# A schedule model with a clock for the load queue, an earlier start of the exponentials and a reordered tail, in a two-attention kernel

## Chip, cores, metric

The kernel runs on one core of one Trainium2 chip. The metric is device microseconds (us) of one execution, median over several; lower is better. Engines: PE is TensorE's matmul and PEld its weight load, ACT is ScalarE, DVE is VectorE, POOL is GpSimd, SP is SyncE, which issues most DMAs.

## The reference

Two independent attentions over 2048 tokens, width 512, 32 heads of 16; the two outputs are concatenated.

```python
# A: attention with a compressive memory, in 4 segments of 512 tokens
phi = lambda t: jnp.where(t > 0, t + 1.0, jnp.exp(t))
g = _sigmoid(beta).reshape(1, H, 1, 1)             # one gate per head
for s in range(N):
    logits = qs @ ks^T * scale + causal_mask       # within the segment
    a_dot = softmax(logits) @ vs
    a_mem = (phi(qs) @ M) / (phi(qs) @ z + 1e-6)   # memory of earlier segments
    outs.append(g * a_mem + (1.0 - g) * a_dot)
    M, z = M + phi(ks)^T @ vs, z + sum(phi(ks))
# B: plain attention, all 2048 keys, no mask; then a @ wo_a and b @ wo_b, concatenated
```
(Shortened: the einsums are written as products.)

## The kernel before

The stream that matters is: scores on PE into two alternating PSUM tiles (`s_ps`, of 3 and 2 banks) → exponential on ACT (`pT`, 749 tiles) → causal mask on GpSimd where needed → accumulation on PE (`acc`). A further 124 blocks of exponentials go to DVE (`vx`). All other work, called chores (projections, phi, memory products, normalisation, output), is fitted into that stream by a Python scheduler *while the program is being built*. It keeps a clock for each engine (`T`), and with it decides which instruction is written next; each engine then runs them in that order. So a constant of the model, such as `SWITCH` (us that PE loses between kinds of matmul), can change the order of the program.

```python
SWITCH = 0.095
ARRIVE = dict(wv=13.0, wk=15.3, wq=16.5, xb=(20.5, 26.0, 31.5, 37.0), wvb=24.0)
T = dict(pe=0.0, act=0.0, dve=0.0, pool=0.0)
# ...
def load_beta():                                   # the gate's 32 numbers
    bsrc = A_beta.rearrange("(rt j e) -> j rt e", j=4, e=2)
    for j in range(4):
        nc.scalar.dma_start(out=beta_t[32 * j:32 * j + 32, :].rearrange("p (rt e) -> p rt e", e=2),
                          in_=bsrc[j:j + 1].to_broadcast([32, 4, 2]))
# ... head: first weights and x are on their way
load_beta()
ld(nc.sync, 2)                                     # A's value weights, then the rest of its key and query weights
ld(nc.sync, 1, P)
ld(nc.sync, 0, P)
# ... first key and query projection, then
pin(nc.scalar.activation(gcol[:], beta_t[:], ACT.Exp, scale=-1.0))     # the gate exp: waits for beta
pin(nc.scalar.copy(kA[0, 0][:], ps0[0][:]))                            # the first scores wait for this
# ... the main loop
    if now >= rel - 0.03 and not held_back(t):
        scores(t)
        t += 1
        if t == 3:
            later(1.2, gates, prio=1)
        continue
# ... chores with due times; for a key of B:
chore(pos0["b", 0, rt] - LEAD + 3 * ch, counted("k", do_k(...)), after=ARRIVE["xb"][ch], ...)
# ... transposes of phi(k) on SP's queue, modelled as a fixed delay
held["pk"] = T["dve"] + 6.5
chore(d - 3, mem(), 2, after=T["dve"] + 7)
# ... tail
partial(3, ...); partial(2, ...)                   # B's last output: 3 of 4 products, in advance
while len(pvq) > 1:
    assert pv(1, True)                             # accumulations
partial(0, last[:, 0, :])
assert pv(1, True)
partial(1, last[:, 1, :])
# ... 4 transposes OT_b, each with the fourth product
# ... checks: are all softmax sums in range? -> flag; then 4 output copies and DMAs
# ... every engine loads the flag and branches over an exact path
```

## Time and profile before

902.71 us, median of 3 (902.5 to 904.79); the profiled execution, another one of 901.82 us, spans 900.1 us.

The page of the kernel before: the span, each engine's busy time with its share, and the group of the exponentials (line, engine, operation, output and input with shapes, count; busy us, mean ns; idle time ahead of it and what ended most of that).

```profile
span 900.1 us, 18954 instructions
...
PE 866.8 (96%) x7674; PEld 260.2 (29%) x7674; DVE 794.2 (88%) x1359; ACT 868.2 (96%) x779; POOL 152.1 (17%) x327
...
L827 ACT ACTIVATE pT<-s_ps 128x1536 bf16<-128x1536 f32 x749 | 856.8, 1287 | 8.3 <-PE s_ps L109 6.1
```

ACT and PE both show 96%. But 411 of PE's matmuls only fill with zeros, so ACT's exponentials are what bounds the kernel, and time can be won where ACT stands idle. The next view shows where it does: ACT's timeline in the first 30 us (start, duration of a run of like instructions, engine, line, operation, count; in brackets the idle time before it and what ended it).

```profile
13.02 0.21 ACT L1066 ACTIVATE gcol<-beta_t 128x8 f32<-128x8 bf16 x1 [9.66 <-DMA beta_t<-in_A_beta_dram]
13.13 0.57 ACT L1067 CAST kA<-k_ps 128x512 bf16<-128x512 f32 x1
14.41 2.37 ACT L827 ACTIVATE pT<-s_ps 128x1536 bf16<-128x1536 f32 x2 [0.71 <-PE s_ps L109]
18.05 4.74 ACT L827 ACTIVATE pT<-s_ps 128x1536 bf16<-128x1536 f32 x4 [1.27 <-PE s_ps L109]
...
28.21 2.37 ACT L827 ACTIVATE pT<-s_ps 128x1536 bf16<-128x1536 f32 x2 [1.62 <-PE s_ps L109]
```

The gate exp, which needs beta, stands in front of the key copy in ACT's order, and so ACT stands idle for 9.66 us and all scores wait with it, for a load of 64 bytes of data. (Not all of it is lost: PE ends the first projections, which the copy needs too, at about 9.0.) The first exp tile starts at 14.41 and, after more gaps, the ninth at 28.21.

After that ACT hardly rests. The same kernel in wide windows: the window, its length, then busy us (and count) of PE, PEld, DVE, ACT and POOL, granted clock, DMA share and GB/s; the last line sums 30 to 880 us.

```profile
90.00:200.00 110.00, 108.11 (x932) 32.77 (x931) 95.47 (x171) 109.14 (x100) 24.38 (x49) 1.00 0.06 13
...
sum 850.00, PE 833.56 PEld 249.40 DVE 774.57 ACT 846.62 POOL 139.16; mean PE 119.08 PEld 35.63 DVE 110.65 ACT 120.95 POOL 19.88
```

ACT is busy 846.62 of 850 us. The end is a chain of its own. First the last output copies and the flag, in the timeline, then two groups of the branch line (count, duration min/median/max in ns, first and last start in us).

```profile
892.69 0.14 DVE L1175 TENSOR_SCALAR flag<-f_ps 1x1 int32<-1x1 f32 x1 [0.26 <-PE f_ps L109]
892.76 1.29 DVE L1179 CAST osb<-l_ps 128x512 bf16<-128x512 f32 x2
```

```profile
L1294 SPq EVENT_SEMAPHORE  x8: 17/17/17, 898.2 to 898.7; - x8
...
L1294 PEldq COMPARE_BRANCH  x1: 3986/3986/3986, 893.6 to 893.6; - x1
```

The flag comes first, then the last two output copies; PE's branch takes 3.99 us, from 893.6 to 897.6, and the end follows.

### The profile page before, as it was taken

What the parts mean: (1) busy time and instruction counts of PE and PEld (TensorE: products, weight loads), DVE (VectorE), ACT (ScalarE), POOL (GpSimd) and SP (SyncE); (2) the same over time, 40 slices, a digit from 0 to 9 for tenths busy, and PEclk for the clock granted to TensorE, in tenths of its full rate; (3) what the DMA queues carried; (4) which work ended last, traced back from release to release, by engine and by line L of the source; (5) the groups of instructions that cost most, each with busy time, mean ns of one, the idle gap of its engine ahead of it and who ended that gap; (6) DMA issues with size and microseconds to landing.
All of it is one profiled execution on the core that took longest, in us unless ns stands there. A gap on an engine that the chain in (4) does not pass through costs nothing.

```text
span 900.1 us, 18954 instructions
## 1 busy us (share of the span) xinstructions
PE 866.8 (96%) x7674; PEld 260.2 (29%) x7674; DVE 794.2 (88%) x1359; ACT 868.2 (96%) x779; POOL 152.1 (17%) x327
## 2 busy tenths in 40 slices
PE   6999999999999999999999999999999999999996
PEld 2222222232323223222232223223222222222321
DVE  1777789989898998988989999999999899999995
ACT  3899999999999999999999999999999999999994
POOL 4630120411303003030120304002030300000000
PEclk8999999999999999999999999999999999999998
DMA  7700000010000110000000010000000000000001
GB/s 185 143 13 7 24 4 5 7 25 7 7 1 14 36 30 8 1 1 7 1 7 2 25 30 1 1 1 1 2 2 1 19 30 1 2 1 2 1 2 28
DMA packets 35649, 15.47 MB, mean 17 GB/s; under 512 B 27360, under 2 KB 35552, under 8 KB 35552
## 3 DMA queue, kind: packets, MB, share of 16 engines
q1 hardware_dynamic: 33776, 13.78, 6.5%
q8 instruction: 62, 1.02, 0.5%
q10 hardware_dynamic: 1776, 0.40, 0.2%
q14 instruction: 35, 0.29, 0.1%
HBM read 4.20 MB, written 4.19 MB: 9 GB/s over the span
## 4 chain that ended last, share of the span: by engine, by line
PE 42%; ACT 31%; issue 12%; DVE 5%; POOL 2%; DVEq 0%; ACTq 0%; POOLq 0%
ACT pT L827 30%; PE acc L109 19%; PE s_ps L109 11%; PE v_ps L109 7%; POOL pT L837 2%; DVE vx L899 2%; PE o_ps L109 2%; PE k_ps L109 1%; DVE vx L915 1%; ACT ex L284 1%; PE q_ps L109 1%; PE am_ps L109 0%; DVE tT L358 0%; DVE tN L391 0%; POOL qB L259 0%
## 5 line engine op out<-in xcount | busy, mean ns | idle before, releaser
L827 ACT ACTIVATE pT<-s_ps 128x1536 bf16<-128x1536 f32 x749 | 856.8, 1287 | 8.3 <-PE s_ps L109 6.1
L899 DVE TENSOR_SCALAR vx<-v_ps 128x512 uint16<-128x512 f32 x496 | 324.7, 684 | 30.2 <-PE v_ps L109 23.8
L109 PE MATMUL s_ps<-qB,KB 32*128 32x512 bf16 x1552 | 250.7, 382 | 8.9 <-ACT pT L827 5.5
L915 DVE TENSOR_SCALAR vx<-vx 128x2048 uint16<-128x2048 uint16 x372 | 244.6, 690 | 1.9 <-PE acc L109 0.7
L109 PE MATMUL acc<-vx,VB 128*32 128x512 f16 x1984 | 181.3, 385 | 0.6 <-DVE vx L915 0.3
L109 PE MATMUL v_ps<-qB,KB 32*128 32x512 bf16 x496 | 171.4, 382 | 1.1 <-DVE vx L899 0.5
L837 POOL TENSOR_SCALAR_AFFINE_SELECT pT<-pT 128x256 bf16<-128x256 bf16 (+2 forms) x242 | 104.8, 462 | 306.0 <-ACT pT L827 304.7
L109 PE MATMUL acc<-pT,VB 128*32 128x512 bf16 x1552 | 152.8, 387 | 0.0
L109 PEld LDWEIGHTS <-KB 32*128 32x128 bf16 x2048 | 84.2, 91 | 235.8 <-issue 227.8
L109 PE MATMUL acc<-zeros 128*128 128x512 bf16 x411 | 137.1, 386 | 0.0
L109 PEld LDWEIGHTS <-VB 128*32 128x32 bf16 x3536 | 74.5, 94 | 161.7 <-issue 152.4
L109 PE MATMUL s_ps<-qA,kA 32*128 32x384 bf16 (+3 forms) x512 | 54.1, 303 | 7.7 <-ACT kA L1067 4.7
L109 PEld LDWEIGHTS <-zeros 128*128 128x128 bf16 x433 | 35.1, 98 | 84.9 <-issue 77.0
L259 POOL TENSOR_SCALAR qA<-qc,par 128x512 bf16<-128x512 bf16 x24 | 16.5, 701 | 248.6 <-DVE qc L257 248.6
L358 DVE STREAM_TRANSPOSE tT<-acc 128x512 f32<-128x512 f32 x64 | 45.0, 704 | 10.2 <-PE acc L109 9.9
L109 PE MATMUL acc<-pT,vA 128*32 128x256 bf16 (+3 forms) x512 | 32.5, 305 | 1.2 <-DVE vx L899 0.8
L109 PEld LDWEIGHTS <-kA 32*128 32x128 bf16 x512 | 17.1, 92 | 47.8 <-issue 39.7
L259 POOL TENSOR_SCALAR qB<-qc,par 128x512 bf16<-128x512 bf16 x32 | 23.6, 750 | 8.6 <-DVE qc L257 8.6
L435 DVE CAST osb<-o_ps 128x512 bf16<-128x512 f32 x28 | 19.2, 687 | 6.6 <-PE o_ps L109 6.3
L304 DVE CAST vA<-v_ps 128x512 bf16<-128x512 f32 x16 | 11.0, 689 | 11.7 <-PE v_ps L109 11.7
L257 DVE CAST qc<-q_ps 128x512 bf16<-128x512 f32 x28 | 19.2, 684 | 2.4 <-PE q_ps L109 2.1
L109 PE MATMUL k_ps<-xT_a,w_a 128*128 128x512 bf16 x64 | 19.6, 383 | 0.8 <-DMA xT_a<-in_A_x_dram 0.7
(88 smaller groups left out, 419.1 us busy)
## 6 DMA issues: line engine op xcount, KB each, us to landing
out_dram<-osb SPq DMA_DIRECT2D x31, 128.0 KB, 1.7
w_b<-in_B_wqkv_dram SPq DMA_DIRECT2D x3, 512.0 KB, 5.2
phk<-phkT SPq DMA_TRANSPOSE x48, 2.3
w_a<-in_A_wv_dram SPq DMA_DIRECT2D x1, 512.0 KB, 6.6
wo_a<-in_A_wo_dram SPq DMA_DIRECT2D x1, 512.0 KB, 4.3
wo_b<-in_B_wo_dram SPq DMA_DIRECT2D x1, 512.0 KB, 5.1
w_a<-in_A_wk_dram SPq DMA_DIRECT2D x1, 384.0 KB, 7.9
w_a<-in_A_wq_dram SPq DMA_DIRECT2D x1, 384.0 KB, 8.5
```

What stands on the lines that cost most here:

```text
L109: return pin(nc.tensor.matmul(out, lhsT, rhs, **k))
L257: pin(nc.vector.tensor_copy(qc[:], ps[:]))
L259: pin(nc.gpsimd.tensor_scalar(dst[:, e, :], qc[:], par[:, e:e + 1], 0.0, ALU.mult, ALU.add))
L284: pin(nc.scalar.activation(ex[:], src, ACT.Exp))
L304: pin(nc.vector.tensor_copy(dst, ps[:].rearrange("p (h d) -> p h d", d=DH)))
L358: pin(nc.vector.transpose(st["tT"][:, e].rearrange("p c d -> p (c d)"), acc[:]))
L435: pin(nc.vector.tensor_copy(osb[:], ps[:]))
L827: pin(nc.scalar.activation(pT[:, 0:n, :], pt[:, 0:n, :], ACT.Exp, scale=SCALE))
L837: pin(nc.gpsimd.affine_select(out=blk, in_=blk, compare_op=ALU.is_ge, fill=0.0, base=0, pattern=[[0, len(sls)], [1, P]], channel_multiplie ...
L899: pin(nc.vector.tensor_scalar(x[:, j, :], vt[:], XSCALE, float(LADDER[0]), ALU.mult, ALU.add))
L915: pin(nc.vector.tensor_scalar(p[:], x[:], float(off - LADDER[0]), 32767.0, ALU.add, ALU.min))
```

## The change

Its intent: give the scheduler a clock for SP's load queue, so that phi of keys and projections wait for the transposes they need rather than for a fixed delay (`T["sp"]`, `on_sp`); make the key projections of B, except those of its first row tile, due 6 tile places earlier (`KLEAD`); give DVE fewer exponentials when it is behind (`VLATE`); let a normalisation go to GpSimd when the model allows; load beta once, contiguous and behind all of A's weights, and put the gate exp behind six exp tiles; load the second row tile's key and query weights ahead of the value weights; in the tail, put all partial output products ahead of the last two accumulations, and the checks behind the output copies.

```diff
-ARRIVE = dict(wv=13.0, wk=15.3, wq=16.5, xb=(20.5, 26.0, 31.5, 37.0), wvb=24.0)
+ARRIVE = dict(w1=11.0, wv=13.5, wk=16.0, wq=17.0, xb=(20.0, 27.0, 33.0, 39.0), wvb=23.0)
-    T = dict(pe=0.0, act=0.0, dve=0.0, pool=0.0)
+    T = dict(pe=0.0, act=0.0, dve=0.0, pool=0.0, sp=SPLOADS)
@@ load_beta
-        for j in range(4):
-            nc.scalar.dma_start(out=beta_t[32 * j:32 * j + 32, :]...)
+        nc.sync.dma_start(out=beta_a[:], in_=A_beta.partition_broadcast(P))
+    def spread_beta():                     # four small copies on GpSimd, beta_a -> beta_t
@@ head: order of loads
-        load_beta()
-        ld(nc.sync, 2)
-        ld(nc.sync, 1, P)
-        ld(nc.sync, 0, P)
+        ld(nc.sync, 1, P, 2 * P)
+        ld(nc.sync, 0, P, 2 * P)
+        ld(nc.sync, 2)
+        ld(nc.sync, 1, 2 * P)
+        ld(nc.sync, 0, 2 * P)
+        load_beta()
@@ projections of A, phi of keys
-                rel = T["pe"] + 10
+                rel = T["sp"] + 3.5
-                held["pk"] = T["dve"] + 6.5
+                held["pk"] = T["sp"] + 2.0
-                chore(d - 3, mem(), 2, after=T["dve"] + 7)
+                chore(d - 3, mem(), 2, after=T["sp"] + 2.5)
@@ keys of B
-                    chore(pos0["b", 0, rt] - LEAD + 3 * ch,
+                    chore(pos0["b", 0, rt] - LEAD - (KLEAD if rt else 0) + 3 * ch,
@@ blocks of exponentials for DVE
+            vmin = VMIN + VLATE * (max(0.0, T["dve"] - T["pe"]) + sum(t["us"] for t in tasks)) / QUAD
-                if u["name"] == "a" or len(u["kbs"]) < VMIN:
+                if u["name"] == "a" or len(u["kbs"]) < vmin:
@@ gate
-        pin(nc.scalar.activation(gcol[:], beta_t[:], ACT.Exp, scale=-1.0))
         pin(nc.scalar.copy(kA[0, 0][:], ps0[0][:]))
-                if t == 3:
-                    later(1.2, gates, prio=1)
+                if t == 6:
+                    pin(nc.scalar.activation(gcol[:], beta_t[:], ACT.Exp, scale=-1.0))
+                    later(1.2, gates, prio=1, ready=on_act(0.2, T["pe"]))
@@ tail
+        (partial 3, 2; accumulations until 2 are left; partial 0, 1; the last 2 accumulations)
-        (checks, flag)          # ahead of the four output copies
+        (checks, flag)          # behind them
@@ ... cut: use of the arrival time w1, GpSimd normalisation, guard on one buffer, bookkeeping of the clocks
```

More of the change, by code (lines that the diff above doesn't have):

```diff
@@ L41 @@
 VMIN = 3
+VLATE = 0.5
 VBACK = 1.5
@@ L58 @@
 POOLMIN = 99
+SPLOADS = 38.0
+SPTRANS = 1.45
+TAILPV = 2
+POOLTT = 1.2
+POOLSLACK = -99.0
+POOLWITH = 1.2
+POOLWAIT = 4.0
 LEAD = 2.5
+KLEAD = 6
 URGENT = 0.0
 START = 8.4
-ARRIVE = dict(wv=13.0, wk=15.3, wq=16.5, xb=(20.5, 26.0, 31.5, 37.0), wvb=24.0)
+ARRIVE = dict(w1=11.0, wv=13.5, wk=16.0, wq=17.0, xb=(20.0, 27.0, 33.0, 39.0), wvb=23.0)
 @with_exitstack
@@ L95 @@
     ports = {k: deque(maxlen=8) for k in ("dve", "pool")}
-    held = {"tT": False, "ex": False, "qc": 0, "phi": deque()}
+    held = {"tT": False, "aT": False, "ex": False, "qc": 0, "phi": deque()}
     def mm(out, lhsT, rhs, at=0.0, **k):
@@ L148, in palloc, with on_sp @@
         return t
+    def on_sp(us, ready):
+        T["sp"] = max(T["sp"], ready) + us
     def mark(key, at=None):
@@ L169 @@
     bd = const.tile([P, 2, P], F32, name="bd")
+    beta_a = const.tile([P, H], BF16, name="beta_a")
     beta_t = const.tile([P, 8], BF16, name="beta_t")
@@ L179, in load_beta @@
     def load_beta():
-        bsrc = A_beta.rearrange("(rt j e) -> j rt e", j=4, e=2)
+        nc.sync.dma_start(out=beta_a[:], in_=A_beta.partition_broadcast(P))
+    def spread_beta():
         for j in range(4):
-            nc.scalar.dma_start(out=beta_t[32 * j:32 * j + 32, :].rearrange("p (rt e) -> p rt e", e=2),
-                              in_=bsrc[j:j + 1].to_broadcast([32, 4, 2]))
+            q = slice(32 * j, 32 * j + 32)
+            pin(nc.gpsimd.tensor_copy(beta_t[q, :].rearrange("p (rt e) -> p rt e", e=2),
+                                      beta_a[q, :].rearrange("p (rt j e) -> p rt j e", j=4, e=2)[:, :, j, :]))
     def head_masks():
@@ L315, in move @@
                 nc.sync.dma_start_transpose(ph[:, kb, :], pk[:, kb * P:(kb + 1) * P])
+            on_sp(4 * SPTRANS, T["dve"] + 0.1)
             if then is not None:
@@ L368, in f @@
             if "aT" not in st:
+                held["aT"] = live[0]
                 st["aT"] = wk.tile([P, 2, 16, 32], F32, name="aT", tag="aT")
@@ L372, in f @@
                 then()
-        later(0.72, f, am)
+        later(0.72, f, am, ok=lambda: "aT" in st if e else not held["aT"])
     def fin_pair(wk, st, name, rt, ridx, ot):
@@ L389, in fin_pair @@
         if aT is None:
-            yield -0.75
-            pin(nc.vector.tensor_tensor(o, tT[:, :, :, 0:DH], rr.to_broadcast(bc), op=ALU.mult))
+            eng = (yield (POOLTT, 0.75)) or nc.vector
+            pin(eng.tensor_tensor(o, tT[:, :, :, 0:DH], rr.to_broadcast(bc), op=ALU.mult))
         else:
@@ L397, in fin_pair @@
             t1, t2 = tT[:, :, :, 0:DH], aT[:, :, :, 0:DH]
-            yield -0.7
-            pin(nc.vector.tensor_tensor(t1, t1, rr.to_broadcast(bc), op=ALU.mult))
-            yield -0.7
-            pin(nc.vector.tensor_tensor(t2, t2, r2[:].to_broadcast(bc), op=ALU.mult))
-            yield -0.7
-            pin(nc.vector.tensor_tensor(o, t1, t2, op=ALU.add))
+            eng = (yield (POOLTT, 0.7)) or nc.vector
+            pin(eng.tensor_tensor(t1, t1, rr.to_broadcast(bc), op=ALU.mult))
+            eng = (yield (POOLTT, 0.7)) or nc.vector
+            pin(eng.tensor_tensor(t2, t2, r2[:].to_broadcast(bc), op=ALU.mult))
+            eng = (yield (POOLTT, 0.7)) or nc.vector
+            pin(eng.tensor_tensor(o, t1, t2, op=ALU.add))
         yield 0.71
@@ L437, in evac @@
             nc.sync.dma_start(out=out2[r0:r0 + P, col0[name]:col0[name] + D], in_=osb[:])
+            on_sp(0.55, T["dve"] + 0.1)
         later(0.69, evac, ps)
@@ L553, in project @@
             def project():
-                rel = T["pe"] + 10
+                rel = T["sp"] + 3.5
                 if (s, rt) != (0, 0):
-                    chore(d - LEAD, part(k()), 4, after=rel if s else ARRIVE["wk"],
+                    chore(d - LEAD, part(k()), 4, after=rel if s else ARRIVE["w1" if rt == 1 else "wk"],
                           key=("k", "a", s, rt), ok=lambda: s == 0 or ("phk", s - 1, rt) in seen)
-                    chore(d - LEAD, part(q()), 4, after=rel if s else ARRIVE["wq"],
+                    chore(d - LEAD, part(q()), 4, after=rel if s else ARRIVE["w1" if rt == 1 else "wq"],
                           key=("q", "a", s, rt))
@@ L566, in load @@
                     xTA[s] = load_xT(wk, "a", s, "xTA", 1)
+                    on_sp(4 * 1.3, T["pe"])
                 vA[s] = wk.tile([P, 4, VROW], BF16, name="vA", tag="vA", bufs=2)
@@ L679, in backlog @@
             return max(0.0, T["dve"] - T["pe"]) + sum(t["us"] for t in runnable() if t["ready"] < T["pe"] + 0.6)
+        ptasks = deque()
         def in_turn(g, prio, end=None):
+            on = [None]
             def step():
-                c = next(g, None)
+                eng = on[0]
+                try:
+                    c = g.send(eng)
+                except StopIteration:
+                    c = None
+                ready = max(T["dve"], T["pool"] + 0.06) if eng else T["dve"]
+                on[0] = None
+                if isinstance(c, tuple):
+                    if T["pool"] < T["pe"] + POOLSLACK and len(ptasks) < 2:
+                        on[0] = nc.gpsimd
+                        ptasks.append((ready, c[0], step))
+                        return
+                    c = -c[1]
                 if c is not None:
-                    later(abs(c), step, prio=prio, ready=T["dve"], port=c < 0)
+                    later(abs(c), step, prio=prio, ready=ready, port=c < 0)
                 elif end is not None:
@@ L692, in pair_end @@
             held["tT"] = False
+            if u["name"] == "a":
+                held["aT"] = False
             if u["sums"] == 30:
@@ L920, in pool_run @@
         def pool_run():
+            while ptasks and max(T["pool"], ptasks[0][0]) < T["pe"] + 0.15:
+                free = sum(t["us"] for t in runnable() if not t["port"] and t["ready"] < T["pe"] + 0.3)
+                if live[0] and free < POOLWITH and T["pe"] < ptasks[0][0] + POOLWAIT:
+                    return
+                ready, us, f = ptasks.popleft()
+                on_pool(us, ready)
+                f()
             while T["pool"] < T["pe"] + 0.1:
@@ L1058 @@
         ps0 = [palloc(mp, [P, W], "k_ps"), palloc(mp, [P, W], "q_ps")]
+        spread_beta()
         live[0] = True
@@ L1133 @@
                 urge()
-        while chores or cur_chore[0] or tasks or len({q["u"]["id"] for q in pvq}) > 1:
+        while chores or cur_chore[0] or tasks or ptasks or len({q["u"]["id"] for q in pvq}) > 1:
             dve_run(T["pe"])
+            pool_run()
             if cur[0] < len(units) - 1 and pv(1, True):
@@ L1154, in partial @@
                    skip_group_check=True)
-        partial(3, mp.tile([P, D], F32, name="l_ps3", tag="misc")[:])
-        partial(2, mp.tile([P, D], F32, name="l_ps2", tag="misc")[:])
-        while len(pvq) > 1:
+        last = [ps_s.tile([P, BANKS[(NT + i) % 2], 512], F32, name="l_ps", tag=f"s{(NT + i) % 2}") for i in range(1)]
+        left = [(3, lambda: mp.tile([P, D], F32, name="l_ps3", tag="misc")[:]),
+                (2, lambda: mp.tile([P, D], F32, name="l_ps2", tag="misc")[:]),
+                (0, lambda: last[0][:, 0, :]), (1, lambda: last[0][:, 1, :])]
+        for n in (1, 1):
+            sb, t = left.pop(0)
+            partial(sb, t())
+        while len(pvq) > TAILPV:
             assert pv(1, True)
-        last = ps_s.tile([P, BANKS[NT % 2], 512], F32, name="l_ps", tag=f"s{NT % 2}")
-        partial(0, last[:, 0, :])
-        assert pv(1, True)
-        partial(1, last[:, 1, :])
+        for sb, t in left:
+            partial(sb, t())
+        while pvq:
+            assert pv(1, True)
         tN = fin[("b", NSEG - 1, NRT - 1)]["tN"]
@@ L1168 @@
                skip_group_check=True)
-        run(sums_ok(wk, 62, 64, okm[:, 2:3], "b"))
-        okb = wk.tile([P, 1], BF16, name="okb")
-        pin(nc.vector.tensor_reduce(okb[:], okm[:], axis=AX.X, op=ALU.min))
-        fps = ps_a.tile([P, W], F32, name="f_ps", tag="misc")
-        mm(fps[0:1, 0:1], ones_b[:], okb[:], start=True, stop=True)
-        flag = const.tile([1, 1], I32, name="flag")
-        pin(nc.vector.tensor_scalar(flag[:], fps[0:1, 0:1], P - 0.5, None, ALU.is_lt))
         for sb in range(4):
@@ L1183 @@
             (nc.scalar if sb == 2 else nc.sync).dma_start(out=out2[r0:r0 + P, D:2 * D], in_=osb[:])
+        run(sums_ok(wk, 62, 64, okm[:, 2:3], "b"))
+        okb = wk.tile([P, 1], BF16, name="okb")
+        pin(nc.vector.tensor_reduce(okb[:], okm[:], axis=AX.X, op=ALU.min))
+        fps = ps_a.tile([P, W], F32, name="f_ps", tag="misc")
+        mm(fps[0:1, 0:1], ones_b[:], okb[:], start=True, stop=True)
+        flag = const.tile([1, 1], I32, name="flag")
+        pin(nc.vector.tensor_scalar(flag[:], fps[0:1, 0:1], P - 0.5, None, ALU.is_lt))
     def exact_problem(name):
```

## The prediction

> **What bounds it.** ScalarE. The page gives ACT 96% busy, 749 exp tiles of 857 us at one line. By stages: ACT works 501.6 of 504 us between 60 and 564 us and 322.1 of 323 between 564 and 887. PE shows 96% too, but part is zero filler. So only ACT's idle time can be won: until its first exp tile (14.41 us), in gaps up to 28 us, and after its last tile (886.95 of a span of 900.1). In between, gaps add up to about 2 us.
>
> **Head.** The waits show ACT idle 9.66 us for beta: the gate exp, ahead of the kA copy in ACT's order, runs at 13.02; first scores 13.75; first tile 14.41. Yet q/k had left PE at 9.0 and qA's first half left DVE at about 9.8. With the gate exp behind six tiles, first scores come at about 9.85, the first tile at 10.5: 3.9 us earlier. Later gaps in the timeline (1.27, 0.40, 0.94, 1.62 us before the tiles at 18.05, 23.18, 25.57, 28.21) come from value projections, masks, and the second row tile's q/k. That q/k now runs right after the first six scores, so the 1.62 us gap should go. But value weights are issued about 1.2 us later.
>
> The new danger is the beta load: behind all of A's weights on SP's queue. The Trainium skill, "DMA: Bandwidth & Descriptors", section "Queues, rings and completion order", says descriptors are consumed in ring order on each DMA engine; this trace agrees (wv lands at 12.6, the last wq piece at 15.7 us). I estimate beta at 16 to 17 us. GpSimd's beta copies wait for it ahead of the first causal masks, so masks start near 17.5 us, the first accumulation near 18.5, tile 7 waits about 1 us, the gate exp not. The ninth tile, at 28.21 before, should start at 22 to 24. Gain: about 5 us.
>
> **Middle.** Counts hardly change: 749 exp tiles and 124 DVE-exponential blocks stay; one normalisation goes from DVE to GpSimd, filler falls by 13. Before, no PE wait for a transpose exceeds 0.7 us, so the queue clock has at most 2 us to win, and reordering can lose as much: 0.
>
> **Tail.** No DVE block is left in the last accumulations, and all 12 partial output projections go ahead of the last two: estimated 0.5 us (the last accumulation started at 888.89). Output copies precede the checks: 1.0 us off the last output's issue (894.2, landing 3.9 later). But the flag comes 1.35 us later after the last transpose. Each engine's branch after it took 3.2 to 4.3 us. The skill, "Runtime: NRT & Kernel Launch", section "Instruction fetch mechanics", explains a taken branch outside the window as an instruction fetch; no run shows the cause, the trace the duration (PE 3.99 us). So flag and branch bind the end: 0.5 to 1 us lost.
>
> **Sum.** 902.7 − 5.3 + 0.5 = 897.8 us after rounding; 8 in 10 between 894.5 and 901.5. Faster by over 2%: 0.01; within: 0.98; slower: 0.01.
>
> **What would show it.** First exp tile near 10.5 us, no ACT wait for beta above 0.5; GpSimd idle from 6.5 to 16–17 us for beta; ninth tile 22–24; last exp tile at 880–883; first to last tile about 871 us (872.5 before); count 749; from last tile to end 13 to 14 us (13.15 before), branches ending last.
>
> **What would make it wrong.** Beta after 19 us: masks, buffers and gate exp then hold ACT microsecond for microsecond. Second row tile's weights later than 12 us. New gaps of over 3 us in the middle, from DVE's changed order. A branch fetch that overlaps otherwise than I think.

## The result, and the profile after

The changed kernel takes 900.2 us (900.09 to 901.49, 4 runs) against 902.79 of the kernel before in the same rounds. The ratio is 0.997, 95% interval 0.9953 to 0.9987. A ratio here is the mean time of one kernel's fast runs over that of the other's of the same rounds, so it is not quite the ratio of the medians. The profiled execution spans 898.4 us.

```profile
span 898.4 us, 18909 instructions
...
PE 860.1 (96%) x7661; PEld 259.4 (29%) x7661; DVE 793.5 (88%) x1358; ACT 868.2 (97%) x779; POOL 156.6 (17%) x331
...
L866 ACT ACTIVATE pT<-s_ps 128x1536 bf16<-128x1536 f32 x749 | 856.1, 1289 | 10.3 <-PE s_ps L118 8.2
```

The totals say little: the same 749 tiles, the same 868.2 us on ACT, and although the wait for beta is gone, the idle time ahead of the exponentials rose from 8.3 to 10.3 us. So the kernel is read by stages. ACT's first 30 us after:

```profile
8.45 0.59 ACT L1113 CAST kA<-k_ps 128x512 bf16<-128x512 f32 x1 [5.12 <-PE k_ps L118]
9.90 6.88 ACT L866 ACTIVATE pT<-s_ps 128x1536 bf16<-128x1536 f32 x6 [0.87 <-PE s_ps L118]
16.67 0.21 ACT L1141 ACTIVATE gcol<-beta_t 128x8 f32<-128x8 bf16 x1
17.22 1.45 ACT L866 ACTIVATE pT<-s_ps 128x1536 bf16<-128x1536 f32 x1 [0.34 <-PE s_ps L118]
21.09 9.22 ACT L866 ACTIVATE pT<-s_ps 128x1024 bf16<-128x1024 f32 x8 [2.42 <-PE s_ps L118]
```

The first tile starts 4.5 us earlier, the gate exp waits for nothing, and the ninth tile, the second of the eight in the last line, starts at 22.01 (28.21 before). GpSimd, which copies beta, waits for it as foreseen, but only until 14.06 us:

```profile
POOL beta_t L198 <- DMA beta_a<-in_A_beta_dram: 7.7, 1, 7.7
```

(Line of the waits: who waited for what, us in total, times, longest.) The order of the loads agrees with the Trainium skill, "DMA: Bandwidth & Descriptors", section "Queues, rings and completion order", by which each DMA engine consumes the descriptors of a ring in order: beta, last of A's loads on SP's queue, lands at 14.0, right after the last query weights at 13.1. It is two to three us earlier than predicted because those weights themselves landed earlier (15.7 before); experiment d1 shows why.

Then the wide windows:

```profile
90.00:200.00 110.00, 106.82 (x914) 33.48 (x910) 97.54 (x178) 107.33 (x99) 25.70 (x50) 1.00 0.06 13
...
sum 850.00, PE 826.07 PEld 247.81 DVE 774.59 ACT 843.33 POOL 138.59; mean PE 118.01 PEld 35.40 DVE 110.66 ACT 120.47 POOL 19.80
```

Between 30 and 880 us ACT works 3.3 us less than before in the same 850 us (843.33 for 846.62), more than half of it in the window from 90 to 200 us. What ACT waited for in these 850 us, after the change (before it was 2.1 us, all for scores):

```profile
ACT pT L866 <- PE s_ps L118: 4.6, 10, 1.4
ACT pT L866 <- PE v_ps L118: 0.5, 2, 0.2
ACT pT L866 <- POOL pT L876: 0.4, 1, 0.4
```

PE is less busy too: nothing became saturated; the two wait for one another more. One example, from the timeline of that stretch:

```profile
110.89 0.69 DVE L320 CAST vA<-v_ps 128x512 bf16<-128x512 f32 x1 [0.45 <-PE v_ps L118]
...
111.64 0.24 PE L118 MATMUL acc<-pT,vA 128*32 128x128 bf16 x4 [0.57 <-DVE vA L320]
...
112.33 2.37 ACT L866 ACTIVATE pT<-s_ps 128x1536 bf16<-128x1536 f32 x2 [1.38 <-PE s_ps L118]
...
```

Read upwards from the last line: ACT waits 1.38 us for scores; on PE the scores stand behind an accumulation that waited 0.57 us for A's values, whose copy on DVE came late because its projection did. In program order the value projections of A's second segment stand at tiles 74, 75, 78 and 80, and at 69, 71, 76 and 77 before. A natural reading is that key projections of B, now due earlier, went ahead of them; experiment a2 speaks against it.

At the end:

```profile
889.50 1.29 DVE L1225 CAST osb<-l_ps 128x512 bf16<-128x512 f32 x2 [0.74 <-ACT osb L1227]
...
891.77 0.14 DVE L1236 TENSOR_SCALAR flag<-f_ps 1x1 int32<-1x1 f32 x1 [0.26 <-PE f_ps L118]
```

```profile
L1347 SPq EVENT_SEMAPHORE  x8: 17/17/17, 896.5 to 897.0; - x8
...
L1347 PEldq COMPARE_BRANCH  x1: 3546/3546/3546, 892.5 to 892.5; - x1
```

The flag now comes after the copies, and the branch, which cannot start before it, ends the program. The Trainium skill, "Runtime: NRT & Kernel Launch", section "Instruction fetch mechanics", says that a taken branch outside the current window forces a fetch of the target page. That fits a record of 3.5 to 4.0 us for one branch; no run here shows that the fetch is what takes it.

Put together, with every stage measured from ACT's records (the tenth exp tile is the first that starts in a steady stream in both; "middle" runs from its start to the start of the last tile):

| us | before | after | difference | predicted |
|---|---|---|---|---|
| start of the first tile | 14.41 | 9.90 | −4.51 | −3.9 |
| start of the tenth tile (head) | 29.56 | 23.34 | −6.22 | −5.3 |
| middle | 856.16 | 860.00 | +3.84 | 0 |
| last tile | 1.23 | 1.05 | −0.18 | |
| end of last tile to end of span (tail) | 13.14 | 14.00 | +0.86 | +0.5 |
| span | 900.09 | 898.41 | −1.68 | |

Head and tail add up to −5.4 us, more than the −4.8 predicted. The middle took 3.84 of it back. (The timed runs give −2.6 us rather than the −1.7 of these two profiles; one execution is good to about 1 us.)

### The profile page after: what moved, and what is told of

It reads as the page before. It is cut to its first block, busy times and chain, and to the rows that moved or that the text cites. A ratio compares the mean times of both kernels' runs of the same rounds, so it can differ in the third digit from the quotient of the medians.

```text
span 898.4 us, 18909 instructions
## 1 busy us (share of the span) xinstructions
PE 860.1 (96%) x7661; PEld 259.4 (29%) x7661; DVE 793.5 (88%) x1358; ACT 868.2 (97%) x779; POOL 156.6 (17%) x331
## 5 line engine op out<-in xcount | busy, mean ns | idle before, releaser
L866 ACT ACTIVATE pT<-s_ps 128x1536 bf16<-128x1536 f32 x749 | 856.1, 1289 | 10.3 <-PE s_ps L118 8.2
L118 PE MATMUL acc<-vx,VB 128*32 128x512 f16 x1984 | 178.0, 385 | 0.4 <-DVE vx L955 0.2
L118 PE MATMUL v_ps<-qB,KB 32*128 32x512 bf16 x496 | 173.2, 382 | 1.3 <-DVE vx L939 0.6
L118 PE MATMUL acc<-zeros 128*128 128x512 bf16 x403 | 133.8, 386 | 0.0
L118 PE MATMUL s_ps<-qA,kA 32*128 32x384 bf16 (+3 forms) x512 | 52.1, 299 | 6.3 <-ACT pT L866 4.7
L275 POOL TENSOR_SCALAR qA<-qc,par 128x512 bf16<-128x512 bf16 x24 | 19.0, 803 | 149.9 <-DVE qc L273 149.9
```

The lines of the kernel that those rows point to most:

```text
L118: return pin(nc.tensor.matmul(out, lhsT, rhs, **k))
L275: pin(nc.gpsimd.tensor_scalar(dst[:, e, :], qc[:], par[:, e:e + 1], 0.0, ALU.mult, ALU.add))
L866: pin(nc.scalar.activation(pT[:, 0:n, :], pt[:, 0:n, :], ACT.Exp, scale=SCALE))
```

## The experiments

Two theories were to be told apart at first: that a head start is *absorbed* later, whatever the order (then nothing was to be won), or that the head start is kept and the *changed order of the middle* costs it. Twelve kernels ran; all give a correct result. "Before" took 902.3 (9 runs), 902.08 (7) and 902.13 (9) us in the three groups.

### a1: the kernel before, with the gate exp moved alone

```diff
 # kernel before
-        pin(nc.scalar.activation(gcol[:], beta_t[:], ACT.Exp, scale=-1.0))
-                if t == 3:
-                    later(1.2, gates, prio=1)
+                if t == 6:
+                    pin(nc.scalar.activation(gcol[:], beta_t[:], ACT.Exp, scale=-1.0))
+                    later(1.2, gates, prio=1, ready=on_act(0.2, T["pe"]))
```

> The kernel before with one edit: the gate exp goes behind the first six exp tiles; beta still comes by its four loads. The order on PE is unchanged. Theory (the beta wait at the head is most of the gain, the rest of the change gives little or takes back): first exp tile near 10.0 us, ninth tile 24 to 25 us (28.2 before, 22.0 in the changed kernel), everything later shifted by the same 3.5 to 4.5 us, time 898.5 to 899.5, so better than the changed kernel. Rival (later stages absorb a head start, the stream being held by DVE or PE): ninth tile just as early, but last tile within 1.5 us of 886.9 and time above 901.

Measured: 896.85 us (896.57 to 897.43), ratio 0.9942 (0.9929 to 0.9956), better than the 898.5 to 899.5 expected; the ninth tile starts at 23.26, not at 24 to 25. PE's program order is that of the kernel before, line for line. ACT's head:

```profile
8.68 0.59 ACT L1066 CAST kA<-k_ps 128x512 bf16<-128x512 f32 x1 [5.33 <-DMA beta_t<-in_A_beta_dram]
...
23.26 7.13 ACT L827 ACTIVATE pT<-s_ps 128x1536 bf16<-128x1536 f32 x6 [1.62 <-PE s_ps L109]
```

The first tile starts at 10.14 and the tenth at 24.61, 4.95 us earlier than before, and the middle takes 856.14 us, against 856.16 before. The head start arrives at the end undiminished: absorption falls. (The first line names beta as what released the copy. The copy does not read beta; the profile infers releasers, and in the changed kernel, where the copy starts at almost the same time, 8.45, it names PE.)

The gain is larger than the 4.27 us of the first tile. While PE had nothing to do before, its clock was taken down, as the windows of the kernel before show (the number after POOL's count is the granted clock):

```profile
9.00:12.00 3.00, 0.03 (x1) 0.00 (x0) 1.41 (x2) 0.00 (x0) 0.00 (x0) 0.85 0.67 210
12.00:15.00 3.00, 1.25 (x7) 0.41 (x8) 0.90 (x5) 1.27 (x3) 0.00 (x0) 0.50 1.06 347
```

The Trainium skill, "TensorE: Matmul & The Clock Gate", "Part 1: The HAM clock gate", gives half clock after about one idle window of 3.4 us. This trace agrees only roughly: finer windows put the fall at 11.11 us, 2.08 us after PE's last matmul, and PE was busy for 0.65 of the 3.41 us before it. In the changed kernel both windows read 1.00. That the lower clock made up the remaining 0.7 us is argued, not shown.

### a2: the changed kernel, key projections of B not earlier

```diff
 # changed kernel
-KLEAD = 6
+KLEAD = 0
```

> The changed kernel with the earlier due time of B's key projections undone (KLEAD 0). Theory: these projections, run at 87 to 97 us ahead of A's value projections, cause the ACT gaps of 1.4 and 0.8 us near 111 to 115 us; without them the excess over the nominal tile rhythm of tiles 60 to 90 falls from 3.9 to about 1.6 us and the time by about 2 us, to 898. Rival (gaps come from the queue clock or from mere reshuffling): gaps of 2 us or more remain between tiles 60 and 90, or as much appears elsewhere, time within 1 us of 900.2.

Measured: 915.83 us (913.95 to 916.99), ratio to before 1.0146 (1.0129 to 1.0162). My theory that the earlier key projections were what cost the time falls as it stood: without them it is 15.6 us worse than with them. (The rival, a time within 1 us of 900.2, misses as well.) ACT's waits from 100 to 210 us:

```profile
ACT pT L866 <- PE s_ps L118: 11.5, 9, 3.2
ACT pT L866 <- PE v_ps L118: 3.6, 1, 3.6
```

In this order B's second key projection stands at tile 82, in the changed kernel at 63. With the rest of the changed schedule the earlier keys are needed. Nor did they push A's values back in the order: without them, the matmuls of the last value projection of the second segment stand behind the same number of score matmuls as in the changed kernel (262 to 265 in both; 246 to 252 in the kernel before). What moved the values stays open.

### a3: the changed kernel, beta loaded early on ACT's queue

```diff
 # changed kernel; the call moves ahead of the weights
-        nc.sync.dma_start(out=beta_a[:], in_=A_beta.partition_broadcast(P))
+        nc.scalar.dma_start(out=beta_a[:], in_=A_beta.partition_broadcast(P))
```

> The changed kernel with the one load of beta issued from ScalarE's queue, right after the two first weight pieces, instead of behind all of A's weights. The order on PE and DVE is unchanged. Theory: GpSimd's wait of 7.7 us for beta delays the causal masks from about 11.5 to 15.5 us, which delays the accumulations (wait for a mask 0.55 us at 18.8), the value projection behind them and so tile 8 (gap 2.4 us). With beta by 6.5 us masks start near 11.5 us and the gap before tile 8 falls to about 1.3 us, the time by about 1 us. Rival (the value cast behind the gate's DVE work alone holds tile 8): gap stays above 2 us, time unchanged.

Measured: 900.42 us, ratio to before 0.998 (0.9966 to 0.9993), so no change against the changed kernel's 900.2. PE's and DVE's orders are those of the changed kernel. The gap ahead of the eighth tile shrank as expected, 2.42 to 1.15 us, but the tenth tile starts at 23.14 against 23.34. The first tile came later, at 11.01, because the matmuls on zeros that warm PE up took longer in this execution (changed kernel, then a3):

```profile
1.46 5.44 PE L118 MATMUL pre<-zeros 128*128 128x512 bf16 x16 [1.46 <-POOL zeros L494]
```

```profile
1.46 6.55 PE L118 MATMUL pre<-zeros 128*128 128x512 bf16 x16 [1.46 <-POOL zeros L494]
```

These same sixteen matmuls took from 5.01 to 6.55 us in the fourteen profiles, without pattern by kernel. So single profiles cannot resolve the head to better than about 1 us; the timed runs, which could, show no gain from an early beta, against the 1 us expected. (The tail of this profile, 14.58 us, is long for a like reason: the granted clock fell to half at 888.0 us, ahead of the last four output products, which took 1.88 us; in the changed kernel it fell at their end, and they took 1.04.)

### a4: the changed kernel, checks and flag ahead of the output copies

```diff
 # changed kernel: the block from run(sums_ok(...)) to the flag moves up
+        run(sums_ok(...)); okb; f_ps; flag
         for sb in range(4):
             ... output copies and DMAs
-        run(sums_ok(...)); okb; f_ps; flag
```

> The changed kernel with the checks and the flag put back ahead of the four output copies, the new order of partial projections kept. Theory: the end is bound by flag, flag load and taken branch (3.5 to 4 us), so the end comes about 1.2 us earlier: last exp tile to end about 12.7 us instead of 14.0, time about 899.0. Rival (the last output transfer binds the end): output copies start 1.0 us later and the end moves later by up to 1 us.

Measured: 898.77 us (898.2 to 899.11), ratio to before 0.9963 (0.9949 to 0.9976); tail 12.70 us against 14.00. PE's order is unchanged.

```profile
L1347 SPq EVENT_SEMAPHORE  x8: 17/17/17, 894.5 to 895.1; - x8
...
L1347 PEldq COMPARE_BRANCH  x1: 3906/3906/3906, 889.9 to 889.9; - x1
```

From the end of the last transpose `OT_b` to the end of the span: 8.34 to 8.36 us in before, a1 and a4, and 9.65 in the changed kernel. So the late flag costs 1.3 us, and the rest of the new tail (the earlier partial products, and no DVE block left among the last accumulations), taken together, is a gain: 12.70 us against 13.14 before. There is a price on the other side, too small to matter: the last outputs overlap the branches, and then take up to 3.9 us to land (in before too), against at most 2.0 in the changed kernel.

### d1: the kernel before, with the gate exp and the second row tile's weights first

```diff
 # a1, and (cut: use of the arrival time w1):
-ARRIVE = dict(wv=13.0, wk=15.3, wq=16.5, xb=(20.5, 26.0, 31.5, 37.0), wvb=24.0)
+ARRIVE = dict(w1=11.0, wv=13.5, wk=16.0, wq=17.0, xb=(20.0, 27.0, 33.0, 39.0), wvb=23.0)
         load_beta()
+        ld(nc.sync, 1, P, 2 * P)
+        ld(nc.sync, 0, P, 2 * P)
         ld(nc.sync, 2)
-        ld(nc.sync, 1, P)
-        ld(nc.sync, 0, P)
+        ld(nc.sync, 1, 2 * P)
+        ld(nc.sync, 0, 2 * P)
```

> The kernel before with the gate exp behind six tiles, and in addition the second row tile's weights loaded first, with the new arrival times in the scheduler; no queue clock, no earlier due time of B's keys, no late limit on DVE blocks, old tail. Theory: the earlier projections of the second row tile let the stream run ahead of the projections that come later; in this build's instruction order B's second key projection stands at tile 81 and A's second-segment values at tiles 73 to 77 (69 to 77 before). So the head is as good as in the changed kernel (tenth tile, number 9 from 0, at about 23 us), but there are ACT gaps of together 3 us or more between tiles 60 and 90, and more to tile 200; two more exp tiles (751) cost another 2.3 us; time 900 to 910. Rival (the late projections of the earlier run without KLEAD come from the queue clock or the limit on DVE blocks, which are not here): excess of tiles 60 to 90 below 2 us and time 896 to 899.

Measured: 906.25 us, ratio to before 1.0054 (1.0031 to 1.0076), with 751 tiles. The head is worse than in a1: tenth tile at 26.07. PE waits 1.7 us for the value weights, after which its granted clock is 0.50 from 16.3 to 19.7 us; and the loads show why the weights are late. The issue lines of d1 and then of the changed kernel (output from input, queue, count, KB each, median us from issue to landing):

```profile
w_a<-in_A_wv_dram SPq DMA_DIRECT2D x1, 512.0 KB, 7.5
...
beta_t<-in_A_beta_dram ACTq DMA_DIRECT2D x4, 0.5 KB, 3.6
```

```profile
w_a<-in_A_wv_dram SPq DMA_DIRECT2D x1, 512.0 KB, 4.2
...
beta_a<-in_A_beta_dram SPq DMA_DIRECT2D x1, 8.0 KB, 5.2
```

With the four small loads of beta on ACT's queue the same 512 KB take 7.5 us; with one contiguous load, 4.2. The windows show the rate (last number, GB/s), d1 and then the changed kernel:

```profile
9.00:12.00 3.00, 2.06 (x13) 0.80 (x13) 1.90 (x3) 2.13 (x3) 0.13 (x1) 1.00 0.41 102
```

```profile
9.00:12.00 3.00, 2.53 (x20) 1.07 (x21) 1.77 (x3) 2.13 (x3) 0.00 (x0) 1.00 1.01 305
```

The strided form costs packets: ACT's queue counts 1776 in d1, 1344 in a3 with the one load, and 1200 in the changed kernel, where beta is not on it; so 576 packets against 144. The Trainium skill, "DMA: Bandwidth & Descriptors", section "Why small descriptors are slow (HBM only)", names a fixed cost per packet and per descriptor; that small ones also slow a neighbour's load by about 3 us is what this pair adds. How they do it is not shown: in the window above, d1's DMA engines were busy only 0.41 of the time, so the packets did not fill them. All fourteen profiles bear it out: the value weights take 6.6 to 7.5 us in the eight kernels with the four small loads, and 4.2 to 5.5 in the six with the one. Among the six is a3, with its one load early and on ACT's queue as before: 4.6. So it is the form of the load (four strided ones or one contiguous), not its queue or place.

The theory that these weights, through the order, bring the gaps between tiles 60 and 90 falls: ACT's idle time there is 1.0 us in d1, against 2.7 in the changed kernel and 0.6 in the kernel before.

### b1: the changed kernel without the queue clock

```diff
 # changed kernel
-                rel = T["sp"] + 3.5
+                rel = T["pe"] + 10
-                held["pk"] = T["sp"] + 2.0
+                held["pk"] = T["dve"] + 6.5
-                chore(d - 3, mem(), 2, after=T["sp"] + 2.5)
+                chore(d - 3, mem(), 2, after=T["dve"] + 7)
```

> The changed kernel with the queue clock taken out again (phi, memory and projection chores wait by the old fixed delays), all else kept. 751 exp tiles instead of 749. Theory (the clock is not the cause of the middle's loss): gaps of 2 us or more between tiles 60 and 90 stay; time within 900 to 904, the two more tiles included. Rival (the clock delays the chores): excess of tiles 60 to 90 falls to about 1.6 us and of 200 to 375 to about 2.6, time 897 to 899 in spite of two more tiles.

Measured: 903.22 us, ratio to before 1.0006 (0.999 to 1.0023), with 751 tiles: 3.0 us more than the changed kernel, and two tiles more are about 2.3 us at 1.16 us each (856.16 us over 739 tiles). The middle is 862.00, or an estimated 859.7 without these two tiles. ACT's idle time between tiles 60 and 90 is 2.2 us, over the 1.6 of the rival. So the losses of the middle stay without the queue clock; taking it out does not bring the order of the kernel before back.

### b3 and b4: a model constant moved by 1%, in the kernel before and in the changed one

```diff
 # b3: kernel before; b4: changed kernel
-SWITCH = 0.095
+SWITCH = 0.096
```

> Control: the kernel before with one constant of the scheduler's model changed by a thousandth of a microsecond (0.095 to 0.096), which reorders the middle and changes nothing on purpose; 749 tiles. If the order of the middle is a lottery: head and tail as before to 0.3 us, tiles 9 to 748 take 1 to 4 us more or less than 856.2. If the middle is robust: within 0.5 us, time 902 to 903.

> Control: the changed kernel with the same constant changed by a thousandth of a microsecond; 752 exp tiles instead of 749. Lottery: time differs from 900.2 by 1 to 5 us, most likely more because of the three more tiles (3.4 us of ScalarE). Robust: within 0.5 us.

This constant is a guess inside the model; moved by 1%, it changes nothing but the order that the scheduler finds. Measured: b3 904.39 us, ratio to before 1.0024 (1.0007 to 1.0041), with 749 tiles; b4 905.26 us, ratio 1.0036 (1.002 to 1.0053), with 752. b3's middle is 859.73 us, 3.6 us longer than before's and almost exactly the changed kernel's 860.00. ACT's waits from 30 to 880 us, before and then b3:

```profile
ACT pT L827 <- PE s_ps L109: 2.1, 7, 0.6
```

```profile
ACT pT L827 <- PE v_ps L109: 2.5, 6, 0.9
ACT pT L827 <- PE s_ps L109: 1.7, 5, 0.7
...
```

(Left out: 0.4 us. Waits of 4.6 us in all for 2.1.) This is the experiment that decides it: in the profiles, a nudge without any content loses as much in the middle as the whole change did. (In the timed runs b3 is about 2.2 us slower than the kernel before, interval 0.6 to 3.7; the profiled execution was the slowest of its four. Its tail, 0.4 us shorter than before's, lies outside the 0.3 expected.) The order of the kernel before is a favourable one, and each of the eight other orders tried here cost time.

### e1: a1 with the new tail order, checks first

```diff
 # a1, and in the tail:
+        (partial 3, 2; accumulations until 2 are left; partial 0, 1; the last 2 accumulations)
```

> The kernel before (its order of the middle kept) with the gate exp behind six tiles, and at the end the changed kernel's order of partial projections, but the checks and the flag ahead of the output copies as before. The best parts alone. Theory: head as in the gate-only run (first tile about 10.1, tile number 9 at about 24.6 us), tiles 9 to 748 in 856.2 us, from the last tile to the end 12.7 instead of 13.1 us; time 0.3 to 0.5 us below the gate-only run, 896.4. Rival (the shorter tail needs that no DVE block is left at the end, which only the late limit of the changed kernel brings): tail 13.0 or more.

Measured: 897.66 us (897.3 to 898.38), ratio to before 0.9953 (0.9939 to 0.9966); no better than a1. The tail is 14.10 us, not the 12.70 of a4. Among its last accumulations there is still one of a DVE block:

```profile
884.59 0.40 PE L110 MATMUL acc<-vx,VB 128*32 128x512 f16 x4
```

The partial products ahead of it delay the last accumulations. From the last exp tile to the last `OT_b` transpose it takes 5.44 us here, 4.79 in before and 4.35 in the changed kernel, where no DVE block is left at the end. So the new tail order costs time when such blocks are left. The limit on late DVE blocks is not the only way to have none: e4 below lacks it, has none left, and takes 3.87 us. And whether the new order gains anything without them is not shown: b3, with the old order and half as many matmuls of DVE blocks after the last exp tile as before (8 for 16), takes 4.36 us. (Another 0.3 us of e1's tail is the clock, which fell to half during the last output products.)

### e2: e1, with the last checks on GpSimd

```diff
 # e1; elementwise checks on GpSimd, the count by a matmul over 34 columns
-        run(sums_ok(wk, 62, 64, okm[:, 2:3], "b"))
-        pin(nc.vector.tensor_reduce(okb[:], okm[:], axis=AX.X, op=ALU.min))
-        mm(fps[0:1, 0:1], ones_b[:], okb[:], start=True, stop=True)
+        (tensor_scalar is_ge, is_le and a product on nc.gpsimd, ahead of the OT_b transposes)
+        mm(fps[0:1, 0:34], ones_b[:], ok1[:, 0, 0:34], start=True, stop=True)
```

> The same, with the last three elementwise checks on GpSimd, beside DVE's last transposes, and the count over the 34 columns by the matmul, so that DVE has two instead of five small instructions ahead of its output copies. Theory (flag, load and branch, or the last output's issue and the branch behind it, bind the end): the flag comes about 0.6 us earlier relative to the last transpose, and the tail is 0.4 to 0.7 us shorter than without, about 12.1 us. Rival (something else binds the end): tail unchanged within 0.15 us.

Measured: 897.59 us, tail 13.81 against 14.10 in e1: 0.3 us in the profile, nothing in the timed runs (897.66 before it). A miss at the low side; and as the granted clock fell 0.35 us later after the last exp tile than in e1, even the 0.3 us may be the clock's.

### e3 and e4: searching a version that beats a1

```diff
 # e3: e1 + second row tile's weights first (as d1) + KLEAD = 6
 # e4: e1 +
-SWITCH = 0.095
+SWITCH = 0.097
```

> The gate-and-tail kernel with the second row tile's weights first and B's keys due earlier, without queue clock and late limit: 747 exp tiles, two fewer. If the order of the middle is a lottery around 860 us for 749 tiles: first to last tile 870 to 875 us, time 895 to 900, so no better than the gate-and-tail kernel. If the two parts help in themselves: first to last tile below 869 us, time below 895.

> Control: the gate-and-tail kernel with the scheduler's constant at 0.097 instead of 0.095, which reorders the middle for no reason and happens to leave 747 exp tiles. Lottery: excess over the nominal tile rhythm after tile 9 of 20 to 24 us instead of 18.0, which eats the 2.3 us of the two tiles; time 896 to 900. Robust: excess 18 us and time 2 us below the gate-and-tail kernel.

Both were chosen because the built order has 747 tiles, two fewer than before, which should save about 2.3 us. Both are worse, and beyond the times expected (895 to 900 and 896 to 900): e3 904.74 us, ratio 1.0027 (1.0012 to 1.0043), e4 908.21 us, ratio 1.006 (1.0044 to 1.0075). ACT's waits in e4, 30 to 880 us:

```profile
ACT pT L828 <- PE s_ps L110: 8.4, 17, 1.6
ACT pT L828 <- POOL qA L260: 3.2, 1, 3.2
...
```

With those left out ACT waits 13.3 us there. Fewer tiles do not make up for such an order. The long waits have a second cost, which the waits alone do not show: PE's granted clock falls in the middle of the run. In e4 (columns as in the wide windows, the granted clock before the last two numbers):

```profile
557.36:564.19 6.83, 5.88 (x46) 1.41 (x45) 4.56 (x9) 3.19 (x3) 3.99 (x6) 0.50 0.01 2
```

PE is busy at half clock, and ACT works 3.19 of 6.83 us.

### All of them

"Middle" as above; "to 749" adds or takes 1.16 us per tile (an estimate). All columns but the last are of one profiled execution; the last is the median of the timed ones, in rounds in which the kernel before took 902.08 to 902.79.

| kernel | tiles | tenth tile | middle | to 749 | tail | median us |
|---|---|---|---|---|---|---|
| before | 749 | 29.56 | 856.16 | | 13.14 | 902.71 |
| a1: gate only | 749 | 24.61 | 856.14 | | 13.13 | 896.85 |
| e1: gate, tail | 749 | 24.83 | 856.15 | | 14.10 | 897.66 |
| e2: checks on GpSimd | 749 | 24.92 | 856.14 | | 13.81 | 897.59 |
| changed | 749 | 23.34 | 860.00 | | 14.00 | 900.2 |
| a3: beta early | 749 | 23.14 | 859.97 | | 14.58 | 900.42 |
| a4: checks first | 749 | 22.72 | 860.00 | | 12.70 | 898.77 |
| b3: before, nudged | 749 | 29.84 | 859.73 | | 12.74 | 904.39 |
| b1: no queue clock | 751 | 23.88 | 862.00 | 859.7 | 14.48 | 903.22 |
| d1: gate, weights | 751 | 26.07 | 863.48 | 861.2 | 13.89 | 906.25 |
| b4: changed, nudged | 752 | 23.31 | 865.54 | 862.1 | 13.51 | 905.26 |
| e3 | 747 | 24.39 | 863.84 | 866.2 | 13.50 | 904.74 |
| e4 | 747 | 24.70 | 869.30 | 871.6 | 12.23 | 908.21 |
| a2: keys not earlier | 749 | 22.64 | 877.39 | | 13.96 | 915.83 |

Kernels with the same order of the middle agree within 0.03 us in it. Nine different orders ran: that of the kernel before is the shortest, and the changed kernel's is among the best of the other eight. Four of the nine hold stretches at half clock in the middle: 17.1 us in a2 and in e4, 6.8 in e3, 3.4 in b1. That costs PE at most half of this time (an estimate: 8.5 us in a2 and e4). The total varies with the clock from execution to execution (e4 takes 905.71 us at a mean clock of 0.993 and 909.74 at 0.988). So the longest middles are not the order's waits alone. The other five orders have no such stretch in the middle; at 749 tiles they take 856.2 to 862.1 us, the kernel before's still the shortest by 3.6.

## Why the prediction was right or wrong

- **The bound.** ACT's exponentials, with time to be won only where ACT is idle: right. Every difference above is ACT waiting or not.
- **Head.** "About 5 us": right in mechanism, somewhat low: −6.22 in the profile. The first tile came at 9.90 (about 10.5 predicted), the ninth at 22.01 (22 to 24), no wait of ACT for beta. Beta came at 14.0 rather than "16 to 17", because I did not count that dropping four small loads speeds up the weights; a1 shows that 4.95 us of the head is the gate exp alone. The seventh tile waited 0.34 us, not 1, and the eighth 2.42.
- **Middle. This is the step that failed**: "Before, no PE wait for a transpose exceeds 0.7 us, so the queue clock has at most 2 us to win, and reordering can lose as much: 0." The term measured +3.84 us. ACT's waits between 30 and 880 us rose from 2.1 to 5.5 us (4.6 for scores, 0.5 for `v_ps`, 0.4 for masks; the longest 1.38), which accounts for 3.4 of it. I had named as a danger single gaps of over 3 us; it was many small ones. The error in the reasoning was to take gain and loss as equally likely: the order before was better than any of the other eight, and a nudge of 1% in a constant (b3) costs 3.6 us in the profile. Leaving such an order has a loss as its expected value, not zero. That it is good because it was picked by trying many is likely, and only argued.
- **Tail.** "0.5 to 1 us lost", "flag and branch bind the end": right: +0.86, of which a4 gives the parts: 1.3 us lost by the late flag, and 0.44 won back ahead of the last transpose. I put that gain down to the earlier partial products and the DVE blocks that are gone from the end; b3 reaches it without the earlier products, so only fewer blocks at the end are supported.
- **Sum.** 897.8 us was predicted, 900.2 measured, within the range, but near its upper end: of the 4.9 us forecast about 2.6 came, and without the 0.9 us that the head gave beyond the forecast it would have been less. The last exp tile ended at 884.4 rather than 880 to 883, and first to last tile took 874.5 us rather than about 871: both the middle again.

What stays open: whether the queue clock, the earlier keys, the limit on late DVE blocks and the normalisation on GpSimd are each worth something. Each of them draws a new order, and the spread of the orders (859.7 to 877.4 us, in part through the halved clock) is larger than any effect one would look for. The limit on late DVE blocks was not undone alone.

The best kernel is a1: three lines of the change, 896.85 us, 5.4 us less than before in the same rounds and 3.3 less than the whole change in others (3.6 less than a3 in its own).

## What to carry to other kernels

Compare two schedules stage by stage at fixed points of the bounding engine (first unit of work, start of the steady stream, last unit, end) and test each part of a change with the order of the rest kept; a part that pays in the head (here 5 us) can be hidden by what another part does to the middle. Where a program's order comes from a model at build time and has been tuned, touching any input of the model draws a new order, so price that in as a loss and nudge a meaningless constant once to learn its size. In an in-order engine put nothing that waits for a small load ahead of work that others wait for; load small tables in one contiguous piece; and decide a flag before the last outputs when a slow branch follows it.

## What the Trainium skill lacked or had wrong

- "Runtime: NRT & Kernel Launch" tells of a fetch at a taken branch but gives no duration; "Advanced Engine Details and Errata", section "Control Flow Timing", gives about 108 ns for compare-and-branch. Here the records of ACT, DVE, POOL and SP are 45 to 72 ns, but PE's is 3546 to 3986 ns, and the other engines' next instruction starts 3.2 to 4.3 us after theirs.
- "DMA: Bandwidth & Descriptors" gives the cost of small descriptors for the transfer that has them, and no figure for a transfer on another queue: beside four strided 0.5 KB loads on another queue, a 512 KB weight load took 6.6 to 7.5 us rather than 4.2 to 5.5 (eight kernels against six).
- No page that I found tells that DMAs in flight beside such branches land late: the slowest of the last outputs took 3.5 to 3.9 us in the nine profiles where the flag came ahead of the output copies, and at most 2.0 in the five where it came behind (a correlation).
- "TensorE: Matmul & The Clock Gate" puts the rise to full clock at about 4 us of matmuls, ±500 ns from run to run (it also says that the phase of a free-running window decides); here it came 2.8 to 6.0 us after the first matmul, and sixteen warm-up matmuls took 5.01 to 6.55 us, in fourteen profiles of one execution each.
- No page speaks of how much an order that a model picks at build time is worth: nine orders of the same work differ by 21 us in the middle of 856 to 877 us (five without a halved clock there by 6, at 749 tiles), and 1% on one model constant moves it by 3.6.
